# Linear attention and a gated feed-forward block: other queues for the last group's output transfers, a last copy in two halves, a new order of the last group's products

## The chip, the cores and the metric

The kernel runs on one core of one Trainium2 chip. A core has TensorE (matrix products), VectorE, ScalarE, GpSimd and SyncE (SP). SP, ScalarE and GpSimd can each issue DMA transfers. The engines have separate instruction lists and wait for each other through semaphores. The metric is the device time of one execution in microseconds; the median of three runs before the change is 297.43 (297.36 to 297.45).

## What is computed

The inputs are q, k, v of shape 8 x 8 x 576 x 64 (batch, heads, sequence, head dimension) and three weight matrices. First comes linear attention with phi(x) = elu(x) + 1, then a gated feed-forward block over 4608 tokens of width 512:

```
kv  = einsum('bhsd,bhse->bhde', phi(k), v);  z = sum over s of phi(k)
num = einsum('bhsd,bhde->bhse', phi(q), kv)
den = einsum('bhsd,bhd->bhs', phi(q), z) + 1e-6
x   = num / den, as 4608 x 512
out = (silu(x @ w_gate) * (x @ w_val)) @ w_out      # inner width 1536
```

## The kernel before

The 4608 tokens are worked in 9 groups of 512 (0 to 8). For each group the kernel forms x, layer 1 (gate and value products, silu, their product h, kept transposed in `hT`) and layer 2 (h times w_out). From group 2 on, some or all of both layers use a scheme with seven block products in place of eight: the operands are halved in two directions, sums of blocks are formed on VectorE (`hs` from h, `ws` from w_out), and seven products of half size are added up to the four output blocks.

In layer 2 of a group the seven products are numbered 1 to 7 and each is done for two halves of tokens, `tt` 0 and 1. An order string such as `"60 61 50"` means product 6 for half 0, then for half 1, then product 5 for half 0. A product has six matmuls of 128x128 by 128x256 (over the inner width), and letters name a part of them: a is the first four, c the fifth, d the sixth, e the first five. Products 1, 6, 7 and 4 of a half go to one PSUM bank (X0 for half 0, X1 for half 1), products 2, 3 and 5 to another (X2, V2); `prd` (L439) writes them. Product 6 goes on adding in the bank where product 1 lies, so ScalarE first copies product 1 out (`keep`, L463, to `part`), and the final sums are formed on VectorE with `fin` (L468): bank times a scale plus the kept part, into a half of an output tile `osb`. The output tile `o0` to `o3` is named by 2 x th + tt, and each has two column halves `.0` and `.1`.

Nothing is scheduled on the chip. The function `op` records each operation with the engine it runs on, an estimate of its time, what it reads and what it writes; `program` records all of them (1362), and a list of numbers (`steps`) written into the kernel says in which order they are issued. An engine's own instruction list is the part of that order which falls to it. Waits between engines are put in by the framework from the tiles that are read and written.

The output of group 8, the last, is written in 16 transfers of 64 rows by 256 columns (64 KB), two for each finished half tile: `out_op` (L1007) records them and `put_1` (L1012) issues them. SP issues 13 of them, ScalarE two and GpSimd one. The last result is o3.0, copied out of bank X1 by VectorE (L997). In all other groups the outputs leave on SP, in transfers of 128 KB.

The order of the last group's layer 2 is

```
ORDER[8] = "10c 20c 11c 21c 10d 20d 11d 21d 60 61 50 70 30 40 51 71 31 41"
```

with `10a 11a 20a 21a` ahead of it among the last products of layer 1. Setting `SEED[g]` makes product 2 use another bank (`seed_bank`, L436: V1 for half 0, G1 for half 1); before, no group does so.

Of the kernel before, what the change touches and what calls it, by code (L numbers as in the profile page):

```python
# [13 lines left out]
P = 128  # L14
# [3 lines left out]
def kernel(  # L18
# [420 lines left out]
    def prd(g, n, tt, fs, seeded):  # L439
# [15 lines left out]
        for (i, f) in enumerate(fs):  # L455
            nc.tensor.matmul(out=(z if n in (2, 3, 5) else x)[:, 0:HD], lhsT=left(f), rhs=right(f),  # L456
                             start=(i == 0 and fs[0] == 0 and (n in (1, 5) or n == 2 and not seeded)),
                             stop=(i == len(fs) - 1), skip_group_check=True)
# [9 lines left out]
    def fin(tt, th, ch, i, from_x):  # L468
        (x, z) = l2_banks(tt)
        nc.vector.scalar_tensor_tensor(out=osb[2 * th + tt][:, HD * ch:HD * ch + HD],  # L470
                                       in0=(x if from_x else z)[:, 0:HD], scalar=1.0 / SC, in1=part[:, 2 * i + tt, :],
                                       op0=ALU.mult, op1=ALU.add)
# [484 lines left out]
    def l2_prd(g, n, tt, fs=tuple(range(HF)), done=True):  # L957
# [11 lines left out]
        if n == 1:  # L969
            if sd:  # L970
                op("ACT", 0.3, lambda: copy_half(x, seed_bank(tt)[:, 0:HD], 1.0), [nm(x)], [nm(seed_bank(tt))])
            else:
                op("ACT", 0.3, lambda: keep(tt, 0, True), [nm(x)], [f"part0{tt}"])
        if n == 2:
            if sd:
                op("ACT", 0.3, lambda: copy_half(dst, o1[:, 0:HD], 1.0 / SC), [nm(dst)], [f"o{tt}.0"])
            else:
                op("DVE", 0.34, lambda: fin(tt, 0, 0, 0, False), [nm(z), f"part0{tt}"], [f"o{tt}.0"])
# [6 lines left out]
        if n == 7:  # L985
            op("DVE", 0.34, lambda: fin(tt, 1, 1, 2, True), [nm(x), f"part2{tt}"], [f"o{2 + tt}.1"])
            if last:
                out_op(g, tt, 1, 1, (nc.sync, nc.scalar) if tt else (nc.sync, nc.sync))
        if n == 3:
            op("DVE", 0.34, lambda: fin(tt, 0, 1, 1, False), [nm(z), f"part1{tt}"], [f"o{tt}.1"])  # L990
            if last:
                out_op(g, tt, 0, 1, (nc.sync, nc.gpsimd) if tt else (nc.sync, nc.sync))
            else:
                op("SP", 0.12, lambda: put(g, tt, 0), [f"o{tt}.0", f"o{tt}.1"], [])
        if n == 4:
            if last and tt:
                op("DVE", 0.34, lambda: nc.vector.tensor_scalar(out=o2[:, 0:HD], in0=x[:, 0:HD], scalar1=1.0 / SC, scalar2=None,  # L997
                                                                op0=ALU.mult), [nm(x)], [f"o{2 + tt}.0"])
                out_op(g, tt, 1, 0, (nc.sync, nc.scalar))
# [7 lines left out]
    def out_op(g, tt, th, ch, engs=(nc.sync, nc.sync)):  # L1007
        for e in range(2):
            eng = {id(nc.sync): "SP", id(nc.scalar): "ACT", id(nc.gpsimd): "POOL"}[id(engs[e])]
            op(eng, 0.06, lambda e=e: put_1(g, tt, th, ch, e, engs[e]), [f"o{2 * th + tt}.{ch}"], [])  # L1010
# [127 lines left out]

    def program():
# [21 lines left out]
        0 1 4 14 15 9 17 18 10 5 20 21 23 6 24 26 27 16 29 3 19 30 32 8 2 33 35 36 7 22 38 28 41 25 39 40 42 31  # L1161
        34 44 45 43 37 47 63 46 48 64 49 105 66 12 50 67 69 106 65 70 51 11 72 68 73 52 75 71 13 76 114 78 77 79
        74 81 80 82 84 53 83 85 54 87 86 88 90 55 89 91 107 93 56 94 92 96 95 57 97 99 98 100 58 102 59 101 103
        113 127 104 60 129 108 128 109 131 117 171 133 110 132 130 135 112 115 137 134 139 111 136 125 138 120
        141 116 143 119 142 145 140 118 122 147 146 144 150 124 126 148 153 121 162 151 156 61 165 155 154 123
        168 62 149 152 163 167 158 176 164 157 172 177 169 159 179 166 170 178 160 181 161 197 180 342 199 182
        200 343 183 198 202 184 204 201 206 203 174 207 185 209 208 205 211 186 210 214 215 173 212 218 220 219
        213 222 175 221 187 223 225 216 224 227 217 229 228 188 230 285 226 232 231 189 234 236 235 237 233 240
        242 238 241 245 243 246 239 248 190 247 250 244 249 252 251 253 276 255 191 254 257 256 259 277 192 258
        193 260 262 261 264 194 267 265 268 263 271 266 273 269 272 274 270 284 298 275 300 278 280 299 302 279  # L1170
        301 286 281 304 303 282 306 288 308 305 287 310 307 296 309 289 312 283 314 313 311 316 290 291 318 317
        315 293 321 319 324 322 297 292 333 326 336 294 325 334 195 339 327 328 347 329 196 320 348 504 323 340
        335 338 350 330 341 337 349 331 352 368 332 353 370 354 369 371 355 373 372 375 356 295 377 357 378 380
        379 376 382 381 358 385 386 351 383 389 344 387 391 393 390 392 394 374 384 396 359 398 397 388 400 360
        399 401 395 403 456 405 402 404 407 345 408 406 411 409 413 346 412 361 416 410 414 417 419 415 418 421
        364 423 422 424 420 426 425 362 428 430 429 447 431 363 365 448 427 433 432 435 438 436 439 434 442 437
        444 440 443 445 441 455 469 446 471 449 470 450 473 457 451 475 452 474 472 477 459 476 479 453 478 481
        467 480 454 462 483 458 485 484 460 487 482 464 486 489 488 498 461 491 501 490 366 468 492 505 499 493
        367 507 494 500 506 496 510 508 495 512 466 502 463 515 503 509 517 497 513 465 516 523 514 518 525 519
        511 527 529 524 528 540 526 542 541 545 543 531 547 546 629 550 530 552 548 551 554 532 553 556 544 558  # L1180
        555 561 557 559 563 562 549 566 560 564 568 567 570 565 569 533 572 571 574 573 577 620 579 575 578 582
        580 576 584 534 586 583 588 585 587 590 589 593 581 591 595 594 598 621 521 600 596 602 601 603 599 535
        606 592 604 608 607 611 597 605 612 609 520 614 613 615 536 617 616 522 618 628 610 642 537 619 644 622
        643 624 646 632 623 648 625 626 645 650 635 647 652 649 627 654 651 653 637 656 633 658 634 657 660 655
        700 630 662 661 671 659 663 640 631 674 664 672 641 666 667 677 665 675 679 636 678 682 668 680 684 639
        669 670 687 638 689 688 701 694 538 685 691 696 690 702 683 539 698 673 676 681 686 706 695 703 715 697
        699 717 716 704 720 707 722 721 725 718 708 705 727 726 723 729 728 731 709 719 733 730 736 732 734 738
        737 724 741 739 743 742 745 710 804 744 747 735 749 746 752 748 750 754 753 740 757 755 751 759 758 761
        711 756 763 760 762 765 764 768 712 770 766 769 773 713 693 775 771 777 714 778 767 776 781 774 779 783
        782 772 786 780 784 787 692 789 797 788 790 792 798 791 793 785 803 815 795 794 817 796 816 819 799 807  # L1190
        800 821 820 801 818 823 805 825 822 802 827 824 826 810 829 808 831 871 830 806 833 828 812 832 835 834
        844 872 836 809 847 837 845 838 873 850 846 839 852 840 848 851 855 841 849 853 842 857 814 843 854 860
        874 862 811 861 865 858 875 864 867 813 859 863 856 869 876 882 866 891 870 868 893 892 877 896 894 884
        898 897 901 880 883 903 902 905 895 899 907 904 909 906 908 900 912 910 914 913 917 885 911 915 919 918
        921 886 916 923 920 887 922 925 924 928 878 930 929 933 926 879 881 935 934 931 937 936 888 939 927 938
        941 944 940 889 932 946 890 945 942 949 951 947 950 953 979 952 955 954 943 957 960 980 956 962 948 961
        958 965 968 963 959 969 966 971 972 970 967 974 964 973 975 977 978 981 976 989 990 991 992 993 983 996
        982 998 1000 997 1002 984 1004 999 985 1011 994 1003 1006 1001 1013 988 995 1015 987 1014 1007 1017 1012
        1016 986 1005 1019 1047 1018 1021 1008 1020 1023 1009 1022 1026 1024 1028 1010 1027 1025 1048 1031 1029
        1033 1049 1032 1030 1036 1034 1050 1038 1037 1035 1051 1041 1039 1052 1043 1042 1040 1045 1053 1044 1060  # L1200
        1046 1062 1061 1065 1056 1067 1066 1070 1063 1072 1068 1071 1074 1073 1054 1076 1064 1078 1075 1055 1057
        1081 1077 1079 1083 1082 1069 1086 1080 1084 1088 1087 1090 1058 1092 1089 1094 1091 1093 1059 1097 1095
        1099 1098 1085 1102 1096 1100 1104 1103 1106 1101 1108 1105 1107 1110 1109 1148 1113 1111 1115 1114 1118
        1116 1112 1120 1149 1122 1119 1117 1124 1121 1123 1126 1125 1129 1154 1131 1127 1130 1134 1132 1137 1128
        1138 1135 1140 1139 1136 1141 1133 1143 1142 1146 1144 1150 1147 1145 1158 1159 1160 1161 1152 1162 1151
        1165 1167 1169 1153 1166 1171 1173 1168 1170 1180 1174 1172 1175 1182 1156 1181 1155 1184 1183 1157 1186
# [40 lines left out]
```

## Time and profile before

| | before |
|---|---|
| median of the runs | 297.43 us |
| the profiled execution's own time | 297.82 us |
| its span, first to last instruction | 296.0 us |
| TensorE busy | 286.4 us (97%) |
| VectorE busy | 258.6 us (87%) |
| ScalarE busy | 236.3 us (80%) |
| GpSimd busy | 42.5 us (14%) |
| granted clock | 0.998 |
| output transfers of 64 KB on SP | 13, 2.1 us to landing (median) |

The span is what lies between the first and the last instruction of the core; what the device needs before and after makes up the rest of the time. An engine's busy time leaves out the instructions that only wait or issue a transfer. In the timeline a row merges instructions that follow each other; "idle before" names what the engine waited for.

### The profile page before, as it was taken

To read this page: it belongs to the slowest core of one execution; us is meant where nothing else is said; L and a number is where in the kernel's file an instruction comes from. 1 tells how busy PE (TensorE), PEld (TensorE's weight loads), DVE (VectorE), ACT (ScalarE), POOL (GpSimd) and SP (SyncE) were. 2 spreads that over 40 slices of the span, in tenths; PEclk is the share of its full clock that TensorE was granted. 3 is DMA by queue.
4 is the path that set the end of the run, shared out by engine and by line. 5 is a ranking of instruction groups with operands and counts; after the bars stand their busy time and mean duration, and the time that the engine had idled before them with its cause. 6 is when DMAs were issued, how large, how long until landed. Compare 5 with 4: busy or idle time off the path is not lost.

```text
span 296.0 us, 7377 instructions
## 1 busy us (share of the span) xinstructions
PE 286.4 (97%) x2939; PEld 212.9 (72%) x2939; DVE 258.6 (87%) x521; ACT 236.3 (80%) x405; POOL 42.5 (14%) x55
## 2 busy tenths in 40 slices
PE   7899999999999999999999999999999999999991
PEld 5644454454866687668887888788888888788881
DVE  4667889999999998999899999999999999757961
ACT  4773977983998689969999999999986688668830
POOL 8554436500000011000100010000000000000000
PEclk9999999999999999999999999999999999999999
DMA  7999999995598319661960669304140443050014
GB/s 203 193 196 200 205 207 207 196 216 87 81 171 190 64 15 171 162 105 33 147 181 2 105 98 222 61 2 100 44 73 2 99 95 22 2 129 15 0 41 103
DMA packets 41506, 32.92 MB, mean 111 GB/s; under 512 B 16432, under 2 KB 36848, under 8 KB 41472
## 3 DMA queue, kind: packets, MB, share of 16 engines
q0 software_dynamic: 20176, 18.35, 40.7%
q1 hardware_dynamic: 21136, 13.97, 21.0%
q8 instruction: 23, 0.38, 0.5%
q10 hardware_dynamic: 160, 0.13, 0.2%
q14 instruction: 11, 0.09, 0.1%
HBM read 37.75 MB, written 9.44 MB: 159 GB/s over the span
## 4 chain that ended last, share of the span: by engine, by line
issue 50%; PE 43%; DMA 2%; ACT 2%; POOL 1%; POOLq 0%
PE pV L826 7%; PE pX L456 6%; PE pG L826 6%; PE pX L351 5%; PE pX L297 3%; PE pV L297 3%; DMA q<-in_q_dram 2%; PE pG L383 2%; PE pV L383 2%; PE pG L297 2%; PE pV L456 2%; PE pX L826 1%; PE pX L268 1%; PE pV L351 1%; PE pX L187 1%
## 5 line engine op out<-in xcount | busy, mean ns | idle before, releaser
L351 PEld LDWEIGHTS <-wl 128*128 128x128 f16 x414 | 40.3, 98 | 9.6 <-issue 0.2
L456 PEld LDWEIGHTS <-hs 128*128 128x128 f16 x384 | 37.2, 98 | 5.4 <-issue 0.7
L456 PEld LDWEIGHTS <-hT 128*128 128x128 f16 x288 | 27.7, 98 | 5.1 <-DVE hs L425 0.4
L351 PEld LDWEIGHTS <-wg 128*128 128x128 f16 x272 | 26.4, 98 | 5.7
L456 PE MATMUL pX<-ws,hs 128*128 128x256 f16 x240 | 28.8, 273 | 0.1
L826 PE MATMUL pV<-xt,wv 128*128 128x512 f16 x104 | 28.3, 379 | 0.0
L368 ACT ACTIVATE ek<-eq 128x512 f16<-128x512 f32 x34 | 21.3, 625 | 5.3 <-DVE eq L855 5.2
L351 PE MATMUL pV<-xt,wg 128*128 128x256 f16 x168 | 23.9, 273 | 0.0
L826 PE MATMUL pG<-xt,wg 128*128 128x512 f16 x80 | 22.5, 379 | 0.0
L368 ACT ACTIVATE ek<-pV 128x512 f16<-128x512 f32 x34 | 20.3, 597 | 2.7 <-PE pV L351 1.9
L351 PE MATMUL pX<-xs,wl 128*128 128x256 f16 x132 | 19.8, 273 | 0.0
L465 ACT ACTIVATE part<-pX 128x256 f32<-128x256 f32 x40 | 14.3, 386 | 6.4 <-PE pX L456 6.3
L456 PE MATMUL pX<-wo,hT 128*128 128x256 f16 x144 | 19.0, 273 | 0.0
L371 DVE SCALAR_TENSOR_TENSOR r<-pG,rr 128x512 f16<-128x512 f32 x20 | 13.7, 687 | 5.5 <-PE pG L351 5.2
L374 DVE SCALAR_TENSOR_TENSOR hT<-pV,sil 128x512 f16<-128x512 f32 x26 | 17.6, 684 | 0.9 <-PE pV L826 0.3
L425 DVE TENSOR_TENSOR hs<-hT 128x512 f16<-128x512 f16 (+3 forms) x35 | 17.8, 514 | 0.0
L365 ACT ACTIVATE rr<-pX 128x512 f32<-128x512 f32 x27 | 15.9, 598 | 2.4 <-PE pX L351 2.3
L470 DVE SCALAR_TENSOR_TENSOR osb<-pX,part 128x256 f32<-128x256 f32 x32 | 12.9, 419 | 5.2 <-ACT part L465 2.9
L1014 POOL DMA_DIRECT2D out_dram<-osb x1 | 0.6, 562 | 116.8 <-DVE osb L470 116.8
L249 DVE TENSOR_TENSOR qp<-qp,rden 128x768 f16<-128x768 f16 (+3 forms) x19 | 17.2, 906 | 0.0
L826 PEld LDWEIGHTS <-wv 128*128 128x128 f16 x112 | 10.9, 98 | 8.5
L124 ACT ACTIVATE ek<-k 128x1152 f16<-128x1152 f16 x14 | 16.1, 1161 | 1.3 <-DMA k<-in_k_dram 1.3
(187 smaller groups left out, 725.2 us busy)
## 6 DMA issues: line engine op xcount, KB each, us to landing
out_dram<-osb SPq DMA_DIRECT2D x64, 128.0 KB, 2.9
k<-in_k_dram POOLq DMA_DIRECT2D x7, 576.0 KB, 7.4
q<-in_q_dram POOLq DMA_DIRECT2D x7, 576.0 KB, 8.9
v<-in_v_dram POOLq DMA_DIRECT2D x7, 576.0 KB, 6.3
wg<-in_moe_w_gate_dram POOLq DMA_DIRECT2D x5, 256.0 KB, 9.2
wv<-in_moe_w_val_dram POOLq DMA_DIRECT2D x5, 256.0 KB, 9.8
wo<-in_moe_w_out_dram POOLq DMA_DIRECT2D x2, 512.0 KB, 15.1
out_dram<-osb SPq DMA_DIRECT2D x13, 64.0 KB, 2.1
```

The costliest lines, as they stand in the source:

```text
L124: nc.scalar.activation(out=e[:, s, :], in_=src[ix(b)][:, s, :], func=AF.Exp, bias=0.0, scale=1.0)
L249: nc.vector.tensor_tensor(out=qv, in0=qv, in1=rden[:, HL * j0:HL * j1].unsqueeze(2).to_broadcast([P, HL * (j1 - j0), D]), op=ALU.mult)
L297: nc.tensor.matmul(out=ps[:, :], lhsT=src[:, i, P * fb:P * fb + P], rhs=xT[i][g % 2][:, :], start=(i == 0), stop=(i == 3))
L351: nc.tensor.matmul(out=dst[:, HN * e:HN * e + HN], lhsT=lhs, rhs=rhs, start=(n in (1, 5) and e == 0 and c == 0), stop=(c == 1), skip_group ...
L365: nc.scalar.activation(out=dst, in_=halves(src), func=AF.Copy, bias=0.0, scale=scale)
L368: nc.scalar.activation(out=dst, in_=src, func=AF.Silu, bias=0.0, scale=1.0)
L371: nc.vector.scalar_tensor_tensor(out=dst, in0=halves(src), scalar=SC, in1=b, op0=ALU.mult, op1=op1)
L374: nc.vector.scalar_tensor_tensor(out=hT[:, fb, :], in0=pv[:, :], scalar=SC, in1=s[:, :], op0=ALU.mult, op1=ALU.mult)
L425: (eng or nc.vector).tensor_tensor(out=o, in0=a, in1=b, op=op)
L456: nc.tensor.matmul(out=(z if n in (2, 3, 5) else x)[:, 0:HD], lhsT=left(f), rhs=right(f), start=(i == 0 and fs[0] == 0 and (n in (1, 5) or ...
L465: nc.scalar.activation(out=part[:, 2 * i + tt, :], in_=(x if from_x else z)[:, 0:HD], func=AF.Copy, bias=0.0, scale=1.0 / SC)
L826: nc.tensor.matmul(out=dst[:, :], lhsT=src[:, i, P * fb:P * fb + P], rhs=xT[i][g % 2][:, :], start=(i == 0), stop=(i == 3))
```

## The change

Five things differ.

- The transfers of the last group are spread by a table `OUTQ`: the first of each pair goes to SP, the second to GpSimd (P) or ScalarE (A). SP has 8, GpSimd 5, ScalarE 3.
- The last copy (o3.0) is two copies of 64 partitions, one recorded for VectorE and one for ScalarE, each followed by its transfer.
- The last group's products have another order, with five matmuls of product 5 ahead of product 6.
- `SEED[8] = 2`: product 2 of the last group goes to the seed bank, and `fin` reads it there; no seed copy is made.
- The list of numbers is new throughout. The operations up to number 1301 are the same; their order on TensorE, SP and for the loads is the same up to the last group, on VectorE and ScalarE it differs in many places.

```diff
-                             start=(i == 0 and fs[0] == 0 and (n in (1, 5) or n == 2 and not seeded)),
+                             start=(i == 0 and fs[0] == 0 and (n in (1, 5) or n == 2 and seeded is not True)),
...
-    def fin(tt, th, ch, i, from_x):
+    def fin(tt, th, ch, i, from_x, own=False):
         (x, z) = l2_banks(tt)
+        if own:
+            z = seed_bank(tt)
...
-            if sd:
+            if sd is True:
                 op("ACT", 0.3, lambda: copy_half(x, seed_bank(tt)[:, 0:HD], 1.0), [nm(x)], [nm(seed_bank(tt))])
...
-                op("DVE", 0.34, lambda: fin(tt, 0, 0, 0, False), [nm(z), f"part0{tt}"], [f"o{tt}.0"])
+                op("DVE", 0.34, lambda: fin(tt, 0, 0, 0, False, sd == 2), [nm(dst), f"part0{tt}"], [f"o{tt}.0"])
...
-                out_op(g, tt, 1, 1, (nc.sync, nc.scalar) if tt else (nc.sync, nc.sync))
+                out_op(g, tt, 1, 1)
...
-                out_op(g, tt, 0, 1, (nc.sync, nc.gpsimd) if tt else (nc.sync, nc.sync))
+                out_op(g, tt, 0, 1)
...
-                op("DVE", 0.34, lambda: nc.vector.tensor_scalar(out=o2[:, 0:HD], in0=x[:, 0:HD], scalar1=1.0 / SC, scalar2=None,
-                                                                op0=ALU.mult), [nm(x)], [f"o{2 + tt}.0"])
-                out_op(g, tt, 1, 0, (nc.sync, nc.scalar))
+                lo, hi = slice(0, C), slice(C, 2 * C)
+                op("DVE", 0.34, lambda: nc.vector.tensor_scalar(out=o2[lo, 0:HD], in0=x[lo, 0:HD], scalar1=1.0 / SC, scalar2=None,
+                                                                op0=ALU.mult), [nm(x)], [f"o{2 + tt}.0a"])
+                op("ACT", 0.3, lambda: nc.scalar.activation(out=o2[hi, 0:HD], in_=x[hi, 0:HD], func=AF.Copy, bias=0.0,
+                                                            scale=1.0 / SC), [nm(x)], [f"o{2 + tt}.0b"])
+                op("SP", 0.06, lambda: put_1(g, tt, 1, 0, 0, nc.sync), [f"o{2 + tt}.0a"], [])
+                op("ACT", 0.06, lambda: put_1(g, tt, 1, 0, 1, nc.scalar), [f"o{2 + tt}.0b"], [])
...
-    def out_op(g, tt, th, ch, engs=(nc.sync, nc.sync)):
-        for e in range(2):
-            eng = {id(nc.sync): "SP", id(nc.scalar): "ACT", id(nc.gpsimd): "POOL"}[id(engs[e])]
-            op(eng, 0.06, lambda e=e: put_1(g, tt, th, ch, e, engs[e]), [f"o{2 * th + tt}.{ch}"], [])
+    OUTQ = {(0, 0, 0): "SP", (0, 0, 1): "SP", (1, 1, 0): "SP", (0, 1, 0): "SP", (1, 0, 0): "SA", (1, 1, 1): "SA", (0, 1, 1): "SP"}
+    QUEUE = {"S": ("SP", 0.6, nc.sync), "A": ("ACT", 0.5, nc.scalar), "P": ("POOL", 0.6, nc.gpsimd)}
+
+    def out_op(g, tt, th, ch):
+        for (e, x) in enumerate(OUTQ[(th, ch, tt)]):
+            op(QUEUE[x][0], QUEUE[x][1], lambda x=x, e=e: put_1(g, tt, th, ch, e, QUEUE[x][2]), [f"o{2 * th + tt}.{ch}"], [])
...
+    ORDER[8] = "10c 11c 20c 21c 10d 11d 50e 20d 21d 60 61 51e 50d 51d 70 71 30 40 31 41"; SEED[8] = 2
...
     steps = """
-        0 1 4 14 15 9 17 18 10 5 20 21 23 6 24 26 27 16 29 3 19 30 32 8 2 33 35 36 7 22 38 28 41 25 39 40 42 31
+        0 1 4 14 15 9 17 18 10 5 20 21 23 6 24 26 27 16 29 2 19 30 32 8 3 33 35 36 7 22 38 28 41 25 39 40 42 31
...
```

In the tuple (th, ch, tt) of `OUTQ`, th and tt name the output tile and ch its column half. The letter pairs "SP" and "SA" stand for SP then GpSimd, and SP then ScalarE.

## The prediction

> **What bounds the kernel now.** I read the page first, for busy shares; then the busy time of each engine in stretches that I chose, to see where TensorE stops being the bound; then the timeline of the last 15 us; then the rows of the output line, for the price of a transfer. The stretches (columns: us, then TensorE, weight loads, VectorE, ScalarE, GpSimd, clock, DMA share, GB/s):
>
> ```profile
> 60.00:281.00 221.00, 220.94 (x2220) 175.65 (x2219) 207.20 (x409) 189.36 (x343) 9.21 (x12) 1.00 0.49 89
> 284.00:290.10 6.10, 6.04 (x54) 5.01 (x52) 2.76 (x8) 1.92 (x5) 0.04 (x1) 1.00 0.34 77
> 290.10:296.03 5.93, 0.00 (x0) 0.00 (x0) 0.40 (x1) 0.00 (x0) 0.52 (x1) 0.88 0.41 100
> ```
>
> TensorE sets the pace up to 290.04 (busy 220.94 of 221.00 us). After it come six microseconds of nearly nothing but transfers. So two things can move the time: TensorE gaps before 290.04, and this tail. The timeline, first around a TensorE gap, then at the end (start, us, engine, line, operation):
>
> ```profile
> 282.43 0.49 PE L456 MATMUL pX<-wo,hT 128*128 128x256 f16 x3
> 282.74 0.66 ACT L465 ACTIVATE part<-pX 128x256 f32<-128x256 f32 x2 [1.55 <-PE pX L456]
> 283.17 1.69 PE L456 MATMUL pX<-ws,hs 128*128 128x256 f16 x14
> ...
> 285.79 0.82 PE L456 MATMUL pX<-wo,hs 128*128 128x256 f16 x6
> 286.52 0.81 PE L456 MATMUL pX<-ws,hT 128*128 128x256 f16 x6
> ...
> 290.06 0.56 POOL L1014 DMA_DIRECT2D out_dram<-osb  x1 [116.75 <-DVE osb L470]
> 290.07 0.42 DVE L997 TENSOR_SCALAR osb<-pX 128x256 f32<-128x256 f32 x1 [0.31 <-PE pX L456]
> 290.53 0.48 ACTq L1014 DMA_DIRECT2D out_dram<-osb  x1
> ```
>
> The last result is copied at 290.50 and ScalarE issues its half at 290.53, but SP is behind. Three narrow windows on SP:
>
> ```profile
> 285.60 1.59 SPq L1014 DMA_DIRECT2D out_dram<-osb  x1
> 292.02 0.55 SPq L1014 DMA_DIRECT2D out_dram<-osb  x1
> 292.65 0.55 SPq L1014 DMA_DIRECT2D out_dram<-osb  x1
> ```
>
> SP issues 13 of the 16 transfers, one per 0.60 to 0.68 us, and its last, for data ready at 290.50, starts at 292.65: a backlog of 2.1 us. One issue took 1.59 instead of 0.55; the DMA view of that stretch shows an "instruction" packet of 16 KB, which runs from 285.50 to 286.81. The same happened at 206.92 (1.32 us, fetch 206.85 to 207.93) and 86.92. I call that the fetch stall. The last transfer lands 2.0 us after its issue, at 294.66, and the span ends 1.37 us later:
>
> ```profile
> L1014 SPq DMA_DIRECT2D out_dram<-osb x1: 547/547/547, 292.7 to 292.7; - x1
> DMA to landing us min/median/max: 2.0/2.0/2.0
> ```
>
> **What the Trainium skill says.** "DMA: Bandwidth & Descriptors", section "Issuing engines are not separate DMA queues": all queues end on the same 16 DMA engines, so a second issuer saves only the sequencer's issue time, "usually small". Here that time is 0.6 us times a queue of 13, and the engines are 0.41 busy in the tail, so it is the larger part. The same page, "Anatomy of one DMA", puts a fixed cost of about 2 us on a transfer, mostly the write receipt; the trace agrees (2.0 us), and no queue removes it. "SBUF — State Buffer", section on the three doors, says GpSimd can't write descriptors while VectorE runs a two-port mode operation; in the tail GpSimd's one issue took 0.56 us beside a PSUM read by VectorE, so no run here shows that.
>
> **The products' order (TensorE).** Before, products 10, 20, 11, 21 end with single matmuls, and product 60 needs bank X0 back after ScalarE's copy of 10. Three matmuls (0.33 us) cover a copy that ends at 283.12, so 60 starts at 283.17, 0.42 after the previous matmul where 0.109 is normal: 0.31 lost. Products 40 and 41 come two places after 70 and 71 and wait for VectorE to empty the bank: 286.52 - 285.79 = 0.73 for six matmuls that need 0.654, so 0.08 lost, twice. After, five matmuls of 50 and two more stand between 10 and 60 (seven, 0.76), and two products stand between 70 and 40. All three waits go: 0.31 + 0.16 = 0.47 us, if the operands are there. They are: 50's first five inputs end at 281.63 and it starts at 282.65; hs1 ends at 282.97 and 60 starts at 283.41; the last sum on VectorE, now hs2's first half, ends near 284.5 (three sums of 0.47 after 283.0) and 70 starts at 283.41 + 2 x 0.654 + 0.76 = 285.48. TensorE ends at 290.04 - 0.47 = 289.57. Product 2 moves to two other PSUM banks; ScalarE empties one with the copy at 280.61 to 281.19; it now comes one place earlier, can start at 280.42 (its input ends at 280.39) and end at 281.00, and the product needs the bank at 281.12. Cost taken: 0, at worst 0.1.
>
> **What becomes late.** The two first results (o0.0, o1.0) leave VectorE after all sums, at 285.15 and 284.82 instead of 283.77 and 284.57. SP's first issue goes from 283.80 to 285.18: harmless alone, since SP has eight issues now.
>
> **The transfers.** Results ready, each product's end plus 0.04 and a copy of 0.42 (VectorE) or 0.38 (ScalarE): o2.1 286.76, o3.1 287.41, o0.1 288.07, o2.0 288.68, o1.1 289.38, o3.0 first half 290.03. SP, one each at 0.68: 285.18, 285.86, 286.79, 287.47, 288.15, 288.83, 289.51, 290.19. Backlog at the end 0.16 instead of 2.1 us. GpSimd issues five, at least 1 us apart but for the first two, 0.56 each; its last near 289.5. Its final drain took 2.73 us and ended at 292.77, 2.15 after its issue; now near 292.2, covered by the landings. ScalarE issues o3.1 at 287.4 (done 288.0, before o2.0's copy at 288.30: cover 0.3), o2.0 at 288.7, and the last half.
>
> **The split copy.** The built order shows what the diff hides: ScalarE's half of o3.0 waits for VectorE's last instruction, not for TensorE. The halves run one after the other: VectorE 289.61 to 290.03, ScalarE 290.06 to 290.45. A half has 64 partitions but the same 256 columns, so I take the full copies' 0.42 and 0.38; the low end would be half of each. So the split costs 0.4 us on the path of the last transfer: issue at 290.48.
>
> **Sum.** 290.48 + 2.0 to 2.4 (transfers of this line issued beside others landed after up to 2.4 us) = 292.5 to 292.9. From the landing to the end: 1.37 before, with four more 0.06 us waits of SP on later semaphores behind it; the last transfer now uses the last-checked semaphore, so 1.13. Span 293.6 to 294.0; middle 293.85, against 296.03: 2.2 us less. The profiled execution took 297.82, the median is 297.43, about 1.4 above the span; the difference carries over: 297.43 - 2.2 = 295.2; I say 295.3, since the rest leans late.
>
> **The rest of the order.** The permutation is new for the whole kernel. TensorE's list is the same until the last group; VectorE's and ScalarE's exchange neighbours in over a hundred places. With TensorE 220.94 of 221.00 us busy there is nothing to gain but 0.2 us (one short wait near 211), and each copy that comes too late costs up to its length. Example: in group 6 a copy of rr from pX, 0.5 from start to start, moves ahead of the table load at 204.20, so what follows is up to 0.5 later. Bounds: -0.2 to +0.6; taken: 0.
>
> **Rivals.** (1) The fetch stall hits SP's first issue. The fetch follows TensorE's instruction count and would come near 285.15; the issue is due at 285.18. If it blocks, the second starts at 286.93 and the eighth at 291.0, lands at 293.0 to 293.4, span 294.2 to 294.6, time 295.6 to 296.0. For it: four issues that began inside a fetch were held until 0.3 to 0.4 after its end; against: an issue 0.02 ahead of one was not (150.34). It decides within 0.1 us. (2) The transfers get in each other's way, three queues writing 64 KB each: landing grows to 3 to 3.7 us, as it did for two transfers beside the fetch; span 294.6 to 295.6, time 296.0 to 297.0. Against: 182 GB/s at the end, and 2.0 to 2.4 us. (3) Slower: the new VectorE and ScalarE order makes TensorE wait for a bank copy in each of groups 2 to 8. At the price of the gap above (0.31) seven give 2.2, which only cancels the gain; it decides at about 0.4 a group, and one 0.6 us copy in front gives 4.2 - 2.2 = 2.0 us slower, 299.4. Against: waits of TensorE on copies are nearly absent now, so there is cover. (4) The change does nothing: excluded if SP's queue is the cause, as the 2.1 us backlog says.
>
> **Chances.** Forecast 0.55; (1) 0.27; (2) 0.08; (3) 0.08; better than 294.9 0.02. The range 294.9 to 296.3 takes in (1) and the hidden 0.6; below and above it lie about 0.18. Faster by over 0.2% (0.6 us, about what can be told apart): forecast, (1), most of (2), 0.90; within: 0.03; slower: 0.07.
>
> **What would show it.** SP's last issue near 290.2 or 291.0; ScalarE's last output copy starting after VectorE's half ends; TensorE's last matmul ending near 289.6 (every 0.1 later is a new wait, and the stretch 60 to 281 tells where); no 0.4 us step before product 60; last landing to end near 1.1. Wrong if the stretch from the last matmul to the end stays near 6 us, or if TensorE ends after 290.04.

## The result, and the profile after

The changed kernel took 295.37 us (median of four runs, 295.22 to 295.39) against 297.39 for the kernel before beside it: ratio 0.9933, 95% interval 0.9915 to 0.995. Run again later it gave 295.38 and a ratio of 0.993 (0.9916 to 0.9945).

First the stretches of the changed kernel, the last two cut where its last matmul ends (columns as before: us, TensorE, weight loads, VectorE, ScalarE, GpSimd, clock, DMA share, GB/s):

```profile
60.00:281.00 221.00, 221.00 (x2226) 175.70 (x2221) 206.91 (x408) 188.45 (x343) 8.90 (x12) 1.00 0.50 89
284.00:289.61 5.61, 5.61 (x52) 4.79 (x49) 3.19 (x8) 1.81 (x5) 2.17 (x4) 1.00 0.41 108
289.61:293.49 3.88, 0.00 (x0) 0.00 (x0) 0.42 (x1) 0.38 (x1) 0.53 (x1) 1.00 0.45 118
```

TensorE ends at 289.61 instead of 290.04, and the stretch in which it does nothing, the tail, is 3.88 us instead of 6.00 (5.93 in the prediction's table, which starts it at 290.10). So 0.43 us came from TensorE's end and 2.12 from the tail, 2.54 in the span (rounded parts). By the medians the gain is 2.02; why that differs comes below.

Neither part is of one piece. TensorE's first matmul at line 456 and its last, before and after:

```profile
73.92 0.38 PE L456 MATMUL pX<-wo,hT 128*128 128x256 f16 x2
289.76 0.27 PE L456 MATMUL pX<-ws,hT 128*128 128x256 f16 x1
```

```profile
74.03 0.27 PE L456 MATMUL pX<-wo,hT 128*128 128x256 f16 x1
289.34 0.27 PE L456 MATMUL pX<-ws,hT 128*128 128x256 f16 x1
```

From start to start that is 215.84 us before and 215.31 after, so TensorE gained 0.53; by the steps between matmuls 0.45 of it are the three waits in the last group and 0.09 lie near 207 to 212 us. 0.11 of this was given back because this execution reached line 456 later. In the tail, the last issue comes 0.90 after the last matmul's end instead of 2.61 (1.71 gained), its transfer lands 0.07 later after its issue, and from that landing to the end it is 0.47 less.

Second, the timeline of the changed kernel around product 60, where 0.31 us were lost:

```profile
282.68 0.71 PE L456 MATMUL pX<-ws,hs 128*128 128x256 f16 x5
...
282.77 0.66 ACT L465 ACTIVATE part<-pX 128x256 f32<-128x256 f32 x2 [1.15 <-PE pX L456]
...
283.33 0.27 PE L456 MATMUL pG<-wo,hT 128*128 128x256 f16 x1
...
283.44 1.47 PE L456 MATMUL pX<-ws,hs 128*128 128x256 f16 x12
```

The row of 12 is products 60 and 61. It starts 0.11 after the matmul ahead of it, the normal step. Product 10 is copied out in the row at 282.77 while five matmuls of product 50 run. Third, the timeline at the end:

```profile
288.75 2.07 SPq L1022 DMA_DIRECT2D out_dram<-osb  x3
...
289.65 0.42 DVE L1000 TENSOR_SCALAR osb<-pX 64x256 f32<-64x256 f32 x1 [0.23 <-PE pX L456]
289.71 0.53 POOL L1022 DMA_DIRECT2D out_dram<-osb  x1 [0.78 <-DVE osb L472]
290.10 0.38 ACT L1002 ACTIVATE osb<-pX 64x256 f32<-64x256 f32 x1 [1.38 <-DVE osb L1000]
290.51 0.47 ACTq L1022 DMA_DIRECT2D out_dram<-osb  x1
```

The three issues of SP in the first row are its last ones. The releaser in the fourth row is the point that the diff hides: ScalarE's half copy was let go by VectorE's, not by TensorE. Fourth, the rows of the output line between 290.26 and 290.6:

```profile
L1022 SPq DMA_DIRECT2D out_dram<-osb x1: 546/546/546, 290.3 to 290.3; - x1
L1022 ACTq DMA_DIRECT2D out_dram<-osb x1: 474/474/474, 290.5 to 290.5; - x1
DMA to landing us min/median/max: 2.1/2.1/2.1
```

SP's last issue starts at 290.27 instead of 292.65, and ScalarE's at 290.51 is now the last of all.

### The profile page after: what moved, and what is told of

Read it like the earlier page. It is cut to its first block, busy times and chain, and to the rows that moved or that the text cites. A ratio compares the mean times of both kernels' runs of the same rounds, so it can differ in the third digit from the quotient of the medians.

```text
span 293.5 us, 7371 instructions
## 1 busy us (share of the span) xinstructions
PE 286.2 (98%) x2939; PEld 213.0 (73%) x2939; DVE 258.6 (88%) x521; ACT 236.2 (80%) x406; POOL 45.1 (15%) x59
## 4 chain that ended last, share of the span: by engine, by line
PE 95%; DMA 2%; ACT 1%; issue 0%; DVE 0%; POOL 0%; POOLq 0%
PE pX L456 20%; PE pV L351 14%; PE pG L351 12%; PE pX L351 10%; PE pV L828 8%; PE pG L828 7%; PE pV L456 5%; PE pX L297 3%; PE pV L297 3%; DMA q<-in_q_dram 2%; PE pG L383 2%; PE pV L383 2%; PE pG L297 2%; PE pX L828 2%; PE pX L187 1%; PE pX L268 1%
## 5 line engine op out<-in xcount | busy, mean ns | idle before, releaser
L456 PEld LDWEIGHTS <-hs 128*128 128x128 f16 x384 | 37.2, 98 | 5.1 <-issue 0.6
L456 PEld LDWEIGHTS <-hT 128*128 128x128 f16 x288 | 27.7, 98 | 5.0 <-DVE hs L425 0.4
L456 PE MATMUL pX<-ws,hs 128*128 128x256 f16 x240 | 29.1, 273 | 0.0
L1022 POOL DMA_DIRECT2D out_dram<-osb x5 | 2.7, 541 | 110.5 <-DVE osb L472 110.5
L456 PE MATMUL pX<-wo,hT 128*128 128x256 f16 x138 | 18.2, 273 | 0.0
L351 PE MATMUL pG<-xs,wl 128*128 128x256 f16 x100 | 16.9, 272 | 0.0
```

The lines of the kernel that those rows point to most:

```text
L351: nc.tensor.matmul(out=dst[:, HN * e:HN * e + HN], lhsT=lhs, rhs=rhs, start=(n in (1, 5) and e == 0 and c == 0), stop=(c == 1), skip_group ...
```

## The experiments

Every run is compared with the kernel before on the same chip. "Tail" is the time from the end of the last matmul to the end of the span in the profiled execution, and "TensorE from L456" the time from the start of its first matmul at line 456 to the start of its last. These two are the clean measures here: the first matmul at line 456 starts anywhere from 73.50 to 74.29 in the 13 traces, while the time from it on is the same 215.31 in nine of them. "Landing" is the moment when a transfer reports its end. Times are medians.

| run | time | ratio (95%) | TensorE from L456 | last matmul ends | SP's last issue | last landing | tail |
|---|---|---|---|---|---|---|---|
| before | 297.3 to 297.5 | 1 | 215.84 | 290.04 | 292.65 | 294.66 | 6.00 |
| changed | 295.37 | 0.9933 (0.9915–0.995) | 215.31 | 289.61 | 290.27 | 292.58 | 3.88 |
| after_again | 295.38 | 0.993 (0.9916–0.9945) | 215.31 | 289.69 | 290.34 | 292.65 | 3.89 |
| queues_alone | 296.10 | 0.9957 (0.9942–0.9971) | 216.12 | 290.18 | 290.67 | 292.88 | 4.12 |
| queues_gp | 295.88 | 0.9946 (0.9933–0.9958) | 215.85 | 290.14 | 290.63 | 292.85 | 3.95 |
| order_alone | 298.05 | 1.0019 (1.0012–1.0026) | 215.31 | 289.50 | 293.01 | 295.01 | 6.67 |
| old_middle | 295.57 | 0.9933 (0.9919–0.9946) | 215.63 | 289.93 | 290.58 | 292.90 | 3.88 |
| unsplit | 295.03 | 0.9918 (0.9905–0.993) | 215.31 | 289.08 | 289.73 | 291.92 | 3.81 |
| unsplit_again | 295.13 | 0.9926 (0.9912–0.994) | 215.31 | 289.42 | 290.08 | 292.22 | 3.82 |
| unsplit_sa | 295.45 | 0.9933 (0.9919–0.9947) | 215.31 | 289.87 | 290.52 | 292.62 | 4.09 |
| best | 294.94 | 0.9922 (0.9909–0.9934) | 215.31 | 289.34 | 289.99 | 292.07 | 3.64 |
| fetch_late | 295.56 | 0.9937 (0.9922–0.9952) | 215.31 | 289.45 | 290.36 | 292.60 | 4.12 |
| fetch_hit | 295.52 | 0.9942 (0.9929–0.9954) | 215.31 | 289.67 | 290.65 | 292.80 | 4.10 |

My theory: the gain is SP's backlog plus three TensorE waits. The first rival: the gain has other sources, such as the list through the middle, or the fetch stall moving away. One part at a time was put in or taken out.

### The queues alone

The kernel before with the table of queues; old order of products, old list, one whole last copy.

```diff
-    def out_op(g, tt, th, ch, engs=(nc.sync, nc.sync)):
...
+    OUTQ = {(0, 0, 0): "SP", (0, 0, 1): "SP", (1, 1, 0): "SP", (0, 1, 0): "SP", (1, 0, 0): "SA", (1, 1, 1): "SA", (0, 1, 1): "SP",
+            (1, 0, 1): "SA"}
+    QUEUE = {"S": ("SP", nc.sync), "A": ("ACT", nc.scalar), "P": ("POOL", nc.gpsimd)}
+
+    def out_op(g, tt, th, ch, engs=None):
+        for (e, x) in enumerate(OUTQ[(th, ch, tt)]):
+            op(QUEUE[x][0], 0.06, lambda e=e, x=x: put_1(g, tt, th, ch, e, QUEUE[x][1]), [f"o{2 * th + tt}.{ch}"], [])
```

> The kernel before, with the sixteen last transfers spread as in the change (SP 8, GpSimd 5, ScalarE 3); order, products and the single last copy stay. Theory (SP's backlog is what was gained): TensorE still ends at 290.04; the last result is ready at 290.50; SP is free by then, so its last issue and ScalarE's are at 290.5 instead of 292.65, the last landing at 292.6, the span 293.7 to 293.9. Time 295.1 to 295.5, so the whole gain of the change. Rival (the new order of the products is the gain): 297.0 to 297.4. Rival (the new list for the other engines is the gain): 297.0 to 297.4.

Measured: 296.10, a gain of 1.4 (0.9942 to 0.9971) instead of 2.0 or more. SP's backlog (the time from its last data's being ready to its last issue) goes as worked out, but something else came in its place. The timeline of this run:

```profile
287.67 0.55 ACTq L1017 DMA_DIRECT2D out_dram<-osb  x1
287.71 0.82 PE L456 MATMUL pX<-ws,hs 128*128 128x256 f16 x6
288.27 0.38 ACT L465 ACTIVATE part<-pV 128x256 f32<-128x256 f32 x1 [0.63 <-PE pV L456]
...
288.71 0.49 PE L456 MATMUL pV<-wo,hs 128*128 128x256 f16 x3 [0.18 <-ACT part L465]
288.71 0.31 PEld L456 LDWEIGHTS <-hs 128*128 128x128 f16 x3 [0.35 <-issue]
```

ScalarE issues the transfer of o2.0 for 0.55 us, so its copy of product 51 starts at 288.27, and product 31 needs that bank: TensorE starts 0.34 us late (the matmul steps in the trace; the weight loads' row has 0.35 of idle). Also GpSimd's drain, the long instruction with which it ends, ends at 293.29, 0.2 after SP's own last drain (293.09), so it is on the path.

### The same with ScalarE relieved

queues_alone with `(1, 0, 0): "SP"` in place of `"SA"`: the second transfer of o2.0 leaves on GpSimd.

> The kernel before with the new queues alone, but the second transfer of o2.0 issued by GpSimd in place of ScalarE. Theory: in the run with the new queues alone this issue on ScalarE (0.55 us) came ahead of its copy of product 51 and made TensorE wait 0.34 us at 288.26; here that wait is gone and the time is 0.2 to 0.4 lower, 295.7 to 295.9. Rival: the wait has another cause and stays, or GpSimd's later drain takes the gain back: 296.0 to 296.3.

Measured: 295.88, 0.22 below the run before. The timeline of the same place:

```profile
287.94 0.82 PE L456 MATMUL pX<-ws,hs 128*128 128x256 f16 x6
288.14 0.38 ACT L465 ACTIVATE part<-pV 128x256 f32<-128x256 f32 x1 [0.27 <-PE pV L456]
...
288.59 0.60 PE L456 MATMUL pV<-wo,hs 128*128 128x256 f16 x4
```

The copy now starts when product 51 is done (its releaser is TensorE, 0.27 of idle), and the wait is gone. So an issue on ScalarE isn't free when a copy stands behind it. In the changed kernel it is covered, since product 51 ends earlier there. By the tail this run has nearly all that the change has, 3.95 against 6.00 before and 3.88 after; what it lacks is above all TensorE's 0.53 us.

### The order alone

The changed kernel with the transfers on the queues of before (SP 13, ScalarE 2, GpSimd 1) and one whole last copy; new order, new list.

```diff
-    OUTQ = {(0, 0, 0): "SP", (0, 0, 1): "SP", (1, 1, 0): "SP", (0, 1, 0): "SP", (1, 0, 0): "SA", (1, 1, 1): "SA", (0, 1, 1): "SP"}
+    OUTQ = {(0, 0, 0): "SS", (0, 0, 1): "SS", (1, 1, 0): "SS", (0, 1, 0): "SS", (1, 0, 0): "SS", (1, 1, 1): "SA", (0, 1, 1): "SP"}
```

> The changed kernel with the transfers back on the queues of before (SP 13, ScalarE 2, GpSimd 1) and one whole last copy on VectorE; new order of the products and new list stay. Theory (SP's backlog): TensorE ends 0.4 to 0.5 earlier, but the first issue on SP comes at 285.5 instead of 283.8 and thirteen issues of 0.64 follow, so the last is at 293.2 or later: the span is 296.3 to 296.8, no gain or a loss, time 297.4 to 298.2. Rival (the new order of the products is the gain): 295.4 to 296.9.

Measured: 298.05, slower by 0.19% (0.12 to 0.26%). Stretches and timeline:

```profile
289.50:296.16 6.66, 0.00 (x0) 0.00 (x0) 0.42 (x1) 0.00 (x0) 0.56 (x1) 0.79 0.42 99
```

```profile
293.01 0.55 SPq L1021 DMA_DIRECT2D out_dram<-osb  x1
```

TensorE ends at 289.50, the gain of the order is there, and none of it reaches the end: the order delivers its first results at 285.4 instead of 283.8, and the last issue of a queue of 13 then starts at 293.01. Only with the short queue does the earlier end of TensorE count. The two parts are not a sum: queues −1.4, order +0.6, together (with the split) −2.0.

This run also answers for the fetch stall. SP's thirteen issues before and in this run (ns, minimum, median and maximum):

```profile
L1014 SPq DMA_DIRECT2D out_dram<-osb x13: 467/549/1594, 283.8 to 292.7; - x13
```

```profile
L1021 SPq DMA_DIRECT2D out_dram<-osb x13: 467/554/596, 285.4 to 293.0; - x13
```

No issue is held here, and still the last one starts 3.06 us after its data are ready (289.95). So the queue by itself sets the end. But part of the 2.1 us of before was the stall: after the held issue SP's next one started at 287.29, for data that were ready at 286.47. Without the stall it could have started near 286.5, and no later issue would then have waited for data, so an estimate from that trace is 0.8 us for the stall and 1.3 for the queue. In the two runs with the queues alone no issue was held either; their gain contains this part, and no run separates it.

### The list through the middle

The changed kernel with the first 1240 places of the list as before.

```diff
     steps = """
-        0 1 4 14 15 9 17 18 10 5 20 21 23 6 24 26 27 16 29 2 19 30 32 8 3 33 35 36 7 22 38 28 41 25 39 40 42 31
+        0 1 4 14 15 9 17 18 10 5 20 21 23 6 24 26 27 16 29 3 19 30 32 8 2 33 35 36 7 22 38 28 41 25 39 40 42 31
...
```

> The changed kernel, but the list of numbers is that of before up to the last group's second half of layer 1 (the first 1240 places), and the new one after it. Theory (the new list of VectorE and ScalarE through the middle neither gains nor costs): the same as the changed kernel within 0.15, 295.2 to 295.5; TensorE gets the wait near 211 us back (0.2) and loses the one near 207 us (0.16). Rival (the new list is part of the gain): 0.4 or more above 295.37. Rival (the new list hides a loss): 0.4 or more below.

Measured: 0.9933 (0.9919 to 0.9946), the ratio of the changed kernel, and the same tail of 3.88. In the changed kernel one wait of TensorE near 211 went (0.22 us) and a new one came at 207.22 (0.16 us), the place that the prediction gave as an example. Its timeline:

```profile
207.03 0.41 ACT L461 ACTIVATE osb<-pX 128x256 f32<-128x256 f32 x1
207.22 0.10 PEld L212 LDWEIGHTS <-R 128*128 128x128 f16 x1
207.29 0.63 ACT L368 ACTIVATE ek<-pV 128x512 f16<-128x512 f32 x1
...
207.49 0.33 PE L212 MATMUL pX<-id,R 128*128 128x128 f16 x3
```

Here ScalarE empties pX with the copy at 207.03, and TensorE's next product in it goes on at 207.49, after that copy. With the old list the wait at 207 is gone and that at 211 is back. TensorE from L456 takes 0.32 us longer than in the changed kernel. About 0.11 of it is this exchange; the other 0.21 are steps near 146.6 and 171.6 that are longer in this trace alone, not in that of before, where the list is the same up to there. So they are not shown to be the list's. What the list is worth is at most a few tenths, and the medians don't resolve it.

### One whole last copy

The changed kernel with o3.0 copied whole by VectorE, both transfers after it; run twice.

```diff
-                op("DVE", 0.34, lambda: nc.vector.tensor_scalar(out=o2[lo, 0:HD], in0=x[lo, 0:HD], scalar1=1.0 / SC, scalar2=None,
+                op("DVE", 0.34, lambda: nc.vector.tensor_scalar(out=o2[:, 0:HD], in0=x[:, 0:HD], scalar1=1.0 / SC, scalar2=None,
...
-                op("ACT", 0.3, lambda: nc.scalar.activation(out=o2[hi, 0:HD], in_=x[hi, 0:HD], func=AF.Copy, bias=0.0,
-                                                            scale=1.0 / SC), [nm(x)], [f"o{2 + tt}.0b"])
+                op("ACT", 0.0, lambda: None, [], [f"o{2 + tt}.0b"])
```

> The changed kernel with one whole last copy on VectorE (128 partitions) in place of the two halves; both transfers wait for it. Theory (the halves run one after the other, the split costs): ScalarE's last issue goes from 290.51 to about 290.1, SP's stays at 290.27 (bound by the issue before it), so the last landing is 0.2 to 0.3 earlier: time 0.1 to 0.3 less than the changed kernel's 295.37, so 295.1 to 295.3. Rival (the halves are a gain): 0.2 to 0.4 more, 295.5 to 295.8.

> The changed kernel with one whole last copy, once more. Its first run gave 295.03, but its last matmul ended 0.5 us earlier than in the changed kernel, for reasons in the first 50 us; the stretch after the last matmul was only 0.07 shorter. So 295.2 to 295.4 if that start was chance, 294.9 to 295.1 if the whole copy is really better by 0.3.

Measured: 295.03 and 295.13. The timeline of the first run:

```profile
288.92 1.36 SPq L1021 DMA_DIRECT2D out_dram<-osb  x2
289.12 0.42 DVE L1000 TENSOR_SCALAR osb<-pX 128x256 f32<-128x256 f32 x1 [0.23 <-PE pX L456]
289.18 0.53 POOL L1021 DMA_DIRECT2D out_dram<-osb  x1 [0.78 <-DVE osb L472]
289.58 0.47 ACTq L1021 DMA_DIRECT2D out_dram<-osb  x1
```

ScalarE's last issue comes 0.77 after the start of the last matmul (288.81), where the changed kernel needs 1.17: the 0.40 of the split is real at that place. But the tail is only 0.07 shorter (3.81 and 3.82). SP's last issue, 0.15 later at 289.73, lands at 291.92 and GpSimd's drain ends at 292.10: both were just behind the split copy. The medians differ by 0.25 to 0.34, with overlapping intervals. In the two profiled executions what exceeds 0.07 lies in the first 74 us, since TensorE from L456 takes the same 215.31; it is not shown to belong to the edit.

### Clearing the end: two more queues

unsplit_sa: the run unsplit with the second transfer of o1.1 on ScalarE, so that GpSimd ends earlier. best: that, and both transfers of o0.0 on GpSimd (SP 7, ScalarE 4, GpSimd 5).

```diff
-    OUTQ = {(0, 0, 0): "SP", (0, 0, 1): "SP", (1, 1, 0): "SP", (0, 1, 0): "SP", (1, 0, 0): "SA", (1, 1, 1): "SA", (0, 1, 1): "SP"}
+    OUTQ = {(0, 0, 0): "PP", (0, 0, 1): "SP", (1, 1, 0): "SP", (0, 1, 0): "SP", (1, 0, 0): "SA", (1, 1, 1): "SA", (0, 1, 1): "SA"}
```

(In unsplit_sa the first entry stays "SP".)

> The changed kernel with one whole last copy on VectorE, and the second transfer of o1.1 issued by ScalarE in place of GpSimd. Theory: in the run with the whole copy alone, GpSimd's drain (292.10) ended level with SP's last drain (292.07) and was on the path; without its last issue GpSimd's last one is near 288.4 and its drain ends more than 0.7 us earlier, so the end is set by the last landing. SP's last issues no longer stand beside one of GpSimd and take 0.55 in place of 0.73. Together 0.1 to 0.4 us below the run with the whole copy alone: 294.6 to 295.0. Rival: the extra issue holds ScalarE (0.55 us) and the landing sets the end anyway: same as with the whole copy alone, 294.9 to 295.2.

> The run unsplit_sa with both transfers of o0.0 on GpSimd (SP 7, ScalarE 4, GpSimd 5). Theory: in unsplit_sa SP's last transfer used a semaphore that SP checks second, so eight more waits of 0.06 us followed its landing (landing to end 1.34 in place of 0.97). With one transfer fewer on SP the last one gets the semaphore that is checked last, GpSimd's last issue still comes 1 us earlier than in the changed kernel, and landing to end is 0.9 to 1.0; last matmul to end 3.5 to 3.7 in place of 3.88, time 295.0 to 295.2. Rival: the order of the checks has nothing to do with it, landing to end stays near 1.3 and the time near that of unsplit_sa, 295.4.

unsplit_sa missed: 295.45, and a tail of 4.09. GpSimd's drain did end early (291.47), but landing to end took 1.34 us. The trace's rows of SP show why. SP checks the transfers' semaphores in a fixed order, about 0.065 us apart when none has to be waited for. The last transfer had got a semaphore that is checked second of nine, so its own check and seven more came after its landing. Those checks in unsplit_sa, then in best:

```profile
L1251 SPq EVENT_SEMAPHORE  x8: 27/28/28, 292.6 to 293.1; - x8
```

```profile
L1251 SPq EVENT_SEMAPHORE  x1: 28/28/28, 292.1 to 292.1; - x1
```

In best the count of transfers on SP and ScalarE is again that of the changed kernel, and the last one has the semaphore that is checked last: landing to end 0.91, tail 3.64, 0.24 below the changed kernel. The time is 294.94, the lowest of all; its interval overlaps that of the changed kernel, so the tail is the firmer evidence. Its last stretch and its timeline:

```profile
289.34:292.98 3.64, 0.00 (x1) 0.00 (x0) 0.42 (x1) 0.00 (x0) 0.00 (x0) 0.83 0.54 137
```

```profile
288.13 0.53 POOL L1021 DMA_DIRECT2D out_dram<-osb  x1 [0.46 <-DVE osb L472]
...
288.48 1.84 ACTq L1021 DMA_DIRECT2D out_dram<-osb  x3
...
289.38 0.42 DVE L1000 TENSOR_SCALAR osb<-pX 128x256 f32<-128x256 f32 x1 [0.23 <-PE pX L456]
```

GpSimd's last issue is 1.2 us before the end of TensorE; its drain ends at 291.14, under the landings. My other guess for unsplit_sa fell: SP's last issue but one still took 0.72 us in both runs, without an issue of GpSimd beside it. Why it is longer than the others stays open.

### The fetch stall, put on SP's chain

Rival 1 of the prediction didn't happen, by a hair: the fetch ran from 284.53 to 285.45 and SP's first issue started at 285.52. To see whether it would have cost, the fetch was moved by taking warm-up matmuls away at the start.

```diff
-    warm(24, pX[1])
+    warm(17, pX[1])
```

(fetch_late; fetch_hit has 22.)

> The changed kernel with 17 warm-up matmuls at the start in place of 24. TensorE's instruction fetch follows its instruction count, so its last fetch comes 7 matmuls (0.76 us) later, near 285.3 to 286.3, and SP's first issue, 285.52, begins inside it. Theory (the fetch stall of rival 1): that issue takes 1.0 to 1.4 us in place of 0.47, SP's last issue starts 0.3 to 0.8 later, time 295.6 to 296.0. Rival: the fetch doesn't hold the issue, or the chain has slack for it: time within 0.15 of the changed kernel, SP's first issue under 0.6.

> The changed kernel with 22 warm-up matmuls in place of 24. With 17 the fetch moved 2.45 us later (287.00 to 287.94) and held SP's fourth issue until 0.40 after its end. By that, two fewer move it by 0.2 to 0.8: it ends between 285.65 and 286.3, and SP's first issue (near 285.5) begins inside it. Theory: that issue takes 0.6 to 1.2 us in place of 0.47 and ends 0.3 to 0.4 after the fetch, SP's last issue comes 0.1 to 0.5 later, time 295.4 to 295.9. Rival: only issues beside other engines' issues are held; the first keeps 0.47 and the time is that of the changed kernel.

In both the fetch came later than I had worked out, 287.00 to 287.94 and 285.92 to 286.95, and met another issue of SP, the fourth and the second. Timelines narrowed to that issue, of fetch_late, of fetch_hit, and the second issue in the changed kernel:

```profile
287.32 1.03 SPq L1022 DMA_DIRECT2D out_dram<-osb  x1
```

```profile
286.10 1.24 SPq L1022 DMA_DIRECT2D out_dram<-osb  x1
```

```profile
286.04 0.59 SPq L1022 DMA_DIRECT2D out_dram<-osb  x1
```

Each was held until 0.40 and 0.39 us after its fetch ended; the fourth issue took 0.51 in the changed kernel. Of the 0.5 and 0.65 us, 0.24 and 0.22 arrived at the end (tails of 4.12 and 4.10), because the changed kernel's chain has slack to give back: its starts are up to 0.84 apart, and 0.64 after the held issue. The medians are 0.18 and 0.14 above the changed kernel's, in the same direction but within the intervals. So it is shown that a fetch can hold SP's issues here and that this reaches the end, with about half of the 0.3 to 0.7 that the prediction gave rival 1 over its forecast.

That SP's first issue would have been held is not shown. Both held issues followed another one of SP by 0.05 to 0.13 us, and the first one comes after a long pause. In five places of the traces an issue began 0.23 to 0.30 us into a fetch and about 1 us after SP's last one, and took its usual 0.47. The one in the changed kernel, beside a fetch from 207.24 to 208.31:

```profile
207.46 0.47 SPq L479 DMA_DIRECT2D out_dram<-osb  x1
```

Five others after such a pause, but 0.88 to 0.92 into the fetch, were held. In order_alone, old_middle, unsplit and unsplit_sa the very issue in question began inside the fetch, but in its last 0.23 us, and took 0.47.

## Why the prediction was right, point by point

- **Product order, 0.47 us.** Held: by the matmul steps of the two traces the three waits in the last group went, 0.45 us less than before. That TensorE's end came 0.43 earlier agrees with it by chance: it also contains the 0.09 of the list and the 0.11 of the start. The worst case of 0.1 for product 2 is not seen.
- **SP's chain, backlog 2.1 to 0.16.** Held in size: last issue 290.27, predicted 290.19. Its first issue was at 285.52, not 285.18, because VectorE's last sums ran 0.3 later than laid out. The third issue took that back: it waits for o2.1 in any case, and started at 286.88, predicted 286.79. The eight starts are 0.68 apart on average, as taken.
- **GpSimd's drain near 292.2, covered.** Off by 0.4: it ended at 292.62. The last issue came 0.2 later than laid out (289.71), and the drain ended 2.39 after that issue, where I had carried over 2.15. In the traces the drain's end follows the landing of GpSimd's last transfer, by 0.70 us with one transfer (before) and by 0.86 with five (here), so the carried figure was too small by 0.16 and the landing by the rest. It was covered by only 0.1 us (SP's last drain, 292.72). In queues_alone the same drain was not covered.
- **ScalarE's issues have cover.** Held for the changed kernel (0.3). queues_alone shows the price without it: 0.34 us.
- **The split costs 0.4 on the path.** Half right. The half copies run one after the other and take 0.42 and 0.38, so half the partitions saved nothing; the last issue, 290.51, is within 0.03 of the forecast. But undoing the split shortens the tail by only 0.07. The step that failed is to call 0.4 the cost: two other ends stood just behind.
- **Landing and end.** 292.58, within 292.5 to 292.9. Landing to end 0.91, where I had 1.13. Four fewer checks of 0.06 account for the move from 1.37 to 1.13. The other 0.2 lies after SP's second drain (0.98 in before, 0.77 here): VectorE's last drain came 0.38 after SP's last one and took 0.14 in before, 0.03 and 0.02 here. This goes with the new order and list, not with the queues: order_alone has VectorE's drain as early as here, queues_alone and queues_gp as late as before. Why is open. The fixed cost of about 2 us is stated by the Trainium skill ("DMA: Bandwidth & Descriptors", "Anatomy of one DMA") for transfers that GpSimd issues; here it was 1.92 to 2.49 us from issue to landing on all three queues.
- **Sum.** The span was 293.49, below 293.6 to 294.0. The time still fell on 295.3 to 295.4, because the offset failed the other way. I took 1.4 from the profiled span to the median, but each run's own time lies 1.8 to 1.9 above its own span, and the profiled execution of before was just 0.4 slower than its median run. The profiled pair, 2.54 apart, overstates the gain that medians show, 2.02, by the same 0.5. The two errors, 0.36 and 0.5, nearly cancel, so that the number came out this close is in part luck.
- **The list.** Held near 0, by one wait lost and one gained: 0.09 us less on TensorE in the two traces.
- **Rivals.** (1) is described above: not met, which was luck, since SP's first issue came 0.07 us after the fetch's end. The step behind it, a fetch at 285.15, failed by 0.6. That it would have held SP's first issue stays unshown. (2) did not happen: 2.1 us to landing at the end. (3) did not happen: TensorE is busy 221.00 of 221.00 us in the middle. (4) is excluded by the result. The split of before's backlog into queue and stall, which the prediction didn't make, is the estimate above.

## What to carry to other kernels

At the end of a kernel, count the issues per queue after the last input is ready: a chain of 13 at 0.6 us, with one held issue in it, was worth more than all waits of TensorE, and an order that ends TensorE earlier was worth nothing while the queue was the last and began later. When one end is shortened, work out the next two (here a GpSimd drain and the order in which semaphores are checked) before pricing it. An offset between a profiled span and a time must be taken from the same execution; the difference between executions is noise, not part of the offset.

## What the runs showed of the hardware that was not expected

- An instruction fetch held issues of SP, not all of them (five that followed a pause of 1 us kept their 0.47). ScalarE's and GpSimd's issues that began inside the same fetches took their usual time: 0.56 at 287.32 in fetch_late and 0.56 at 286.41 in fetch_hit.
- The fetch doesn't follow the count of matmuls in a simple way: with 24, 22 and 17 warm-up matmuls it began 4.8, 3.5 and 2.2 us before the last matmul started. At 0.11 us a matmul, 0.2 and 0.8 us were to be expected. With 24 it also moved between runs of nearly the same program, from 4.1 to 4.9 in eight traces.
- GpSimd's final drain ended at a nearly fixed time after the landing of GpSimd's last transfer: 0.70 us with one transfer issued near the end (before, order_alone), 0.82 with four (unsplit_sa), 0.86 with five (nine traces), 0.90 with six (queues_gp). From the last issue's end that is 2.1 to 2.5 us. It sets a time by which GpSimd must have issued its last transfer if the end isn't to wait for it.
- The Trainium skill, "DMA: Bandwidth & Descriptors", "Issuing engines are not separate DMA queues", calls the issue time saved by a second issuer usually small. At this kernel's end the measurement decides otherwise: 1.4 to 1.6 us from the queues alone, part of it (0.8 by the estimate above) a held issue that the shorter queue no longer had.
